# Attention values in two half-width banks, and all key-sample maxima computed in the MLP

## The chip, the cores and the metric

The kernel runs on one core of one Trainium2 chip. The metric is the device time of one execution in microseconds (us). A core has five engines that run side by side, each with its own queue of instructions in order: TensorE (PE in the profile; its weight loads are listed as PEld), VectorE (DVE), ScalarE (ACT), GpSimd (POOL) and SyncE (SP), which here only issues transfers (DMAs). Matmul results land in PSUM, eight banks of 128 partitions by 512 float32 values.

## The reference

`x` has 2048 rows (queries, tokens) of 448 channels. Two branches read it, and a gate per token mixes them.

```python
# A: attention, 16 heads of 28 channels, one shared set of keys and values
q = (x @ wq).reshape(B, S, 16, 28).transpose(0, 2, 1, 3)
k, v = x @ wk, x @ wv
p = softmax(einsum("bhqd,bkd->bhqk", q, k) * 28 ** -0.5)
a = einsum("bhqk,bkd->bhqd", p, v).transpose(0, 2, 1, 3).reshape(B, S, 448) @ wo
# B: shift mixing, then an MLP, each with a residual
h = gelu(layernorm(x) @ w1)               # 448 -> 448, its four quarters shifted by +1 -1 +2 -2 tokens
x1 = x + concat(shifted quarters) @ w2
b = x1 + gelu(layernorm(x1) @ w3) @ w4    # 448 -> 1792 -> 448
g = sigmoid((x * gate_w).sum(-1))
out = g * a + (1 - g) * b
```

## The kernel before

All data are float32. Outside the values and the output projection, a matmul of full precision is made of three faster ones, from a "high" and a "low" part of each operand (names that end in `h` and `l`).

The program runs in three stages, and every engine executes its instructions in the order in which the program text emits them (the schedule is manual; the framework only adds the waits).

**Stage 1** projects queries, keys, values and gate, writes the queries to a DRAM tile `qd`, and computes the shift-mixing half of B.

**Stage 2, the MLP.** Four blocks `b` of 512 tokens; in each, 14 chunks `f` of 128 hidden channels. Chunk `f` runs `w3_part` (11 matmuls of 512 columns, L130 to L134; then two gelus on ScalarE, `gh` L625 and `gf` L626; then `gl = gf - gh` on VectorE, L627) and, from f = 2 on, the four `w4_part` calls of chunk f - 2 (12 matmuls of 448 columns, L635 to L637) into four accumulators. At the end of a block the accumulators are added to `x1` (L693). Between the chunks stand other small jobs: splitting weights, loading keys, layernorm of the next block.

**Stage 3, attention.** Sixteen units `u`: 512 queries by four heads, one head in each quarter of the partitions. A unit has eight steps `v`, each over two tiles `kt` of 128 keys. A step does, in this order on TensorE:
- `scores` of both key tiles: each takes four PSUM banks, one for each head, and fills them in three passes (L800). ScalarE turns each bank into `p = exp(...)` (L810);
- in steps 4 to 7 (`WO_AT`) `wo_job`: the output projection of one quarter of the unit before (L763), added on VectorE (L775);
- `values` of the step before: one bank, 16 passes of 512 columns in four rounds of four (L822), added into `o` by VectorE (L826, L828). Row 0 of each head's result is the sum of its exponentials.

The banks form a ring. `take()` takes the one at the head of the list `banks`, and each is appended at its tail when its reader has been emitted, so an instruction that takes a bank waits for the reader of whoever used it eight takes earlier.

**The shift of the exponentials.** Exponentials are taken of scores minus an estimated maximum. For each unit `max_all` multiplies the queries with 32 sampled keys (`khd`, four matmuls, L203) and reduces on VectorE (L204); `max_end` makes a high and a low part of the negative maxima, transposes them (L227) and writes them with eight small DMAs on SyncE's queue into two spare rows of each head in the query tile `qh` (L231), where the scores' matmul picks them up. The maxima of unit 0 are computed in the MLP (the list `fills`, in the last block), those of unit u + 1 in step 2 of unit u, into a bank of the ring.

**Sums and normalisation.** `sums_begin` reads the sums of a unit in step 0 of the next, `recip` inverts them and spreads them through DRAM with two DMAs, `norm` multiplies `o` by them (L753) ahead of the projection. Queries come from `qd` by `q_load` (L178) and are cast and split by `q_split` (L183, L184).

A tail transposes and normalises the last unit, with a few warm-up matmuls in between. A last, conditional part redoes everything with exact maxima if a sum is out of bounds; it isn't entered here.

Of the kernel before, what the change touches and what calls it, by code (L numbers as in the profile page):

```python
# [9 lines left out]
F32 = mybir.dt.float32  # L10
# [6 lines left out]
P = 128  # L17
# [3 lines left out]
DH = 28  # L21
F = 1792
C = D // 4
NB = S // 512
# [12 lines left out]
def f32(ap):  # L37
    return ap.bitcast(F32)
# [3 lines left out]
def gated_mix_kernel(  # L42
# [44 lines left out]
    def misc_tile(name):  # L87
        return psA.tile([P, 512], F32, tag="misc", bufs=1, name=name)
# [86 lines left out]
    def q_load(u, raw):  # L175
        b, g = divmod(u, NG)
        qr_of[u] = raw
        nc.sync.dma_start(raw, qd[g, :, 512 * b:512 * b + 512])  # L178
# [15 lines left out]
    mx_of = {}  # L194
    mc_of = {}

# [22 lines left out]

    def max_end(u):  # L220
        mr = mx_of.pop(u).rearrange("p j t -> p (j t)")
        mc = late.tile([P, 32], F32R, tag="mc", bufs=1, name=f"mc_{u}")
        nc.vector.tensor_scalar(mc[:, 0:16], mr, -1.0, None, op0=ALU.mult)
        nc.vector.scalar_tensor_tensor(mc[:, 16:32], mr, -1.0, f32(mc)[:, 0:16],
                                       op0=ALU.mult, op1=ALU.subtract)
        mrow = late.tile([P, 32], F32, tag="mrow", bufs=1, name=f"mrow_{u}")
        nc.vector.transpose(mrow, f32(mc))  # L227
        for k in range(2):
            for p in range(4):
                r = 32 * p + 16 * k  # L230
                nc.sync.dma_start(  # L231
                    f32(qh_of[u])[DH + k:P:32, :].rearrange("j (t p q) -> p j t q", p=4, q=32)[p], mrow[r:r + 16, :])

# [368 lines left out]
    with tc.tile_pool(name="s2", bufs=1, reuse_waits="tile") as s2, \  # L602
# [4 lines left out]

        fills = [lambda: max_all(0, misc_tile("m_0")), lambda: max_end(0)]

        def fill():  # L610
            if fills:
                fills.pop(0)()

# [25 lines left out]
        for b in range(NB):  # L639
            acc = [ps2.tile([P, 512], F32, tag="acc", bufs=4, name=f"acc_{b}_{t}") for t in range(4)]  # L640
            gs = {}
            for f in range(NF):
# [28 lines left out]
                if b == 2 and f == 1:  # L671
                    nc.gpsimd.memset(f32(khd), 0.0)
                    for j in range(4):
                        nc.sync.dma_start(f32(khd)[32 * j:32 * j + DH, j, :], f32(kH)[0:DH, 0:MK])
                    q_load(0, s2a.tile([P, 512], F32, tag="xn", bufs=1, name="qr_0"))
                if b == 2 and f == 5:
                    q_split(0, qh0, ql0)
                if f >= 2:
                    for t in range(4):
                        w4_part(f - 2, t, gs[f - 2], acc)  # L680
                        if b > 2 and t % 2 == 0 and f < NF - 1:
                            fill()
            for t in range(4):
# [5 lines left out]
            for t in range(4):  # L689
# [3 lines left out]
                nc.vector.tensor_add(xt, xt, acc[t][:, 0:D])  # L693
        assert not fills
    ctx2.close()


    with tc.tile_pool(name="s3", bufs=1, reuse_waits="tile") as s3, \
# [7 lines left out]
        def take():  # L706
            return banks.pop(0)
# [109 lines left out]
        def values(u, v, add=True):  # L817
            pv = take()
            for kt in (2 * v, 2 * v + 1):
                ps = p_of.pop((u, kt))  # L820
                for j in range(4):
                    nc.tensor.matmul(pv[32 * j:32 * j + 32, :], vext[:, kt, :], ps[j],  # L822
                                     start=(kt % 2 == 0), stop=(kt % 2 == 1), tile_position=(0, 32 * j))
            if v == 0:
                o_of[u] = s3.tile([P, 512], F32, tag="o", bufs=2, name=f"o_{u}")
                nc.vector.tensor_copy(o_of[u], pv)  # L826
            elif add:
                nc.vector.tensor_add(o_of[u], o_of[u], pv)  # L828
            else:
                return pv  # L830
            banks.append(pv)

        READ = (0, 1, 2, 3)
        DRAIN = ()
        WO_AT = (4, 5, 6, 7)
        M_AT = 2

        for k in range(NU * NV):
# [6 lines left out]
            for kt in (2 * v, 2 * v + 1):  # L845
                late_exps(u, kt)
            if v == 2 and sums:
                norms.append(recip(*sums.pop()))
            if v == 3 and norms:
                norm(*norms.pop())  # L850
            if v == M_AT and u + 1 < NU:
                ps = take()
                max_all(u + 1, ps)
                banks.append(ps)
                max_end(u + 1)
            job = None
# [7 lines left out]
            if k:  # L864
                values(*divmod(k - 1, NV))
                if v == 0:
                    sums.append(sums_begin(u - 1, o_of[u - 1]))
        assert not sums and not norms

        u = NU - 1  # L870
        pv = values(u, NV - 1, False)
        o = o_of[u]
        on_of[u] = s3.tile([P, 512], F32, tag="on", bufs=2, name=f"on_{u}")
        toks = [slice(t * P, (t + 1) * P) for t in range(4)]
        tp = [bank(f"ot_{i}").rearrange("p (t n) -> p t n", t=4) for i in range(2)]
        tq = [bank(f"oq_{t}")[:, 0:P] for t in range(4)]
        rr = s3.tile([P, 2, 2, 4], F32, name="rr4")
# [33 lines left out]
        def keep_warm(n):  # L911
            for _ in range(n):
                nc.tensor.matmul(banks[0][:, 0:256], warm[:, 0:P], warm, start=True, stop=True)

        for t in range(4):
            nc.vector.tensor_add(o[:, toks[t]], o[:, toks[t]], pv[:, toks[t]])
        with tc.block():
# [34 lines left out]
        with tc.If(again > 0, label="redo"):  # L952
            for b in range(NB):
                for g in range(NG):
# [3 lines left out]
                    max_full(u, bank)  # L958
                    max_end(u)
                    pv = take()  # L960
# [66 lines left out]
```

## Time and profile before

| | |
|---|---|
| median of 3 runs | 971.56 us (971.14 to 971.71) |
| the profiled execution | 970.74 us, its span 968.9 us |
| TensorE busy | 960.1 us, 99% |
| ScalarE busy | 647.0 us, 67% |
| VectorE busy | 345.7 us, 36% |
| stage 2 starts, stage 3 starts | about 127 us, about 402 us |

The span is the time from the first to the last instruction in the trace. The page's groups give a line, the engine, the operation, the tiles written and read, shapes and count, then busy time and the mean length of one in ns, then the idle time of the engine just ahead of these instructions and what ended it. Rows of the timeline give the start, the length, and in square brackets the idle time before with its releaser; rows of several instructions are merged (xN). A row of the windows view has the stretch, the busy time of PE, PEld, DVE, ACT and POOL with the count of instructions, and then the granted TensorE clock, the share of the DMA engines and GB/s. A row of the waits view has the engine and line that waited, what it waited for, the total in us, how often, and the longest. Matmuls are pipelined, so TensorE shows as busy even where it waits for a bank or an operand: its pace is read from the starts.

### The profile page before, as it was taken

To read this page: it belongs to the slowest core of one execution; us is meant where nothing else is said; L and a number is where in the kernel's file an instruction comes from. 1 tells how busy PE (TensorE), PEld (TensorE's weight loads), DVE (VectorE), ACT (ScalarE), POOL (GpSimd) and SP (SyncE) were. 2 spreads that over 40 slices of the span, in tenths; PEclk is the share of its full clock that TensorE was granted. 3 is DMA by queue.
4 is the path that set the end of the run, shared out by engine and by line. 5 is a ranking of instruction groups with operands and counts; after the bars stand their busy time and mean duration, and the time that the engine had idled before them with its cause. 6 is when DMAs were issued, how large, how long until landed. Compare 5 with 4: busy or idle time off the path is not lost. (4 is left out here: it accounts for less than half of the span.)

```text
span 968.9 us, 19222 instructions
## 1 busy us (share of the span) xinstructions
PE 960.1 (99%) x7571; PEld 589.3 (61%) x7571; DVE 345.7 (36%) x636; ACT 647.0 (67%) x1262; POOL 74.9 (8%) x105
## 2 busy tenths in 40 slices
PE   9999999999999999999999999999999999999996
PEld 7788888888888888644444444444444444444442
DVE  5663354433413421233333333333233332333323
ACT  5532444422222222589999999999999999999993
POOL 2242200221002400200000000000000000000000
PEclk9999999999999999999999999999999999999999
DMA  9703342300300300100000010000010000100001
GB/s 317 263 27 76 103 162 83 89 22 10 93 1 1 82 1 1 60 13 14 14 23 14 24 50 24 14 13 24 24 51 15 14 25 13 53 23 2 13 13 42
DMA packets 38753, 46.22 MB, mean 48 GB/s; under 512 B 8880, under 2 KB 27008, under 8 KB 38656
## 3 DMA queue, kind: packets, MB, share of 16 engines
q1 hardware_dynamic: 35632, 39.45, 13.6%
q10 hardware_dynamic: 3024, 5.47, 1.6%
q8 instruction: 61, 1.00, 0.4%
q14 instruction: 36, 0.29, 0.1%
HBM read 32.85 MB, written 11.67 MB: 46 GB/s over the span
## 5 line engine op out<-in xcount | busy, mean ns | idle before, releaser
L810 ACT ACTIVATE p<-bank 128x512 f32<-128x512 f32 x1024 | 510.9, 653 | 42.7 <-PE bank L800 42.7
L822 PE MATMUL bank<-p,vext 128*32 128x512 f32 x2048 | 245.9, 598 | 0.0
L800 PEld LDWEIGHTS bank<-qh,kH 30*128 30x128 f32 x1024 | 86.2, 182 | 141.8 <-ACT p L810 128.4
L800 PE MATMUL bank<-qh,kH 30*128 30x512 f32 x1024 | 168.4, 465 | 0.1
L625 ACT ACTIVATE gh<-g 128x512 fp32r<-128x512 f32 x55 | 32.8, 597 | 187.6 <-PE g L134 187.6
L800 PE MATMUL bank<-qh,kL 28*128 28x512 f32 x1024 | 137.9, 404 | 0.0
L822 PEld LDWEIGHTS bank<-p,vext 128*32 128x32 f32 x2048 | 59.9, 110 | 127.3 <-issue 101.1
L800 PE MATMUL bank<-ql,kH 28*128 28x512 f32 x1024 | 131.3, 389 | 0.0
L828 DVE TENSOR_TENSOR o<-o,bank 128x512 f32<-128x512 f32 x111 | 76.3, 687 | 123.9 <-PE bank L822 72.9
L627 DVE TENSOR_TENSOR gl<-gf,gh 128x512 fp32r<-128x512 f32 x55 | 38.3, 696 | 168.0 <-ACT gf L626 168.0
L636 PE MATMUL acc<-w4l,gh 128*128 128x448 f32 x220 | 80.4, 366 | 0.0
L635 PE MATMUL acc<-w4h,gh 128*128 128x448 f32 x220 | 80.4, 365 | 0.0
L637 PE MATMUL acc<-w4h,gl 128*128 128x448 f32 x220 | 80.3, 365 | 0.0
L800 PEld LDWEIGHTS bank<-ql,kH 28*128 28x128 f32 x1024 | 73.6, 185 | 9.6
L131 PE MATMUL g<-al,w3h 128*128 128x512 f32 x168 | 65.7, 391 | 0.0
L130 PE MATMUL g<-ah,w3h 128*128 128x512 f32 x168 | 65.6, 390 | 0.0
L132 PE MATMUL g<-ah,w3l 128*128 128x512 f32 x168 | 65.6, 390 | 0.0
L800 PEld LDWEIGHTS bank<-qh,kL 28*128 28x128 f32 x1024 | 62.1, 184 | 0.0
L763 PE MATMUL bank<-wof,on 128*32 128x448 f32 x512 | 61.2, 551 | 0.0
L775 DVE SCALAR_TENSOR_TENSOR ot<-bank,gg,ot 128x448 f32<-128x448 f32 x44 | 30.1, 684 | 85.7 <-PE bank L763 56.9
L635 PEld LDWEIGHTS acc<-w4h,gh 128*128 128x128 f32 x220 | 41.3, 188 | 4.7
L902 POOL TENSOR_TENSOR ot<-y,ot 128x448 f32<-128x448 f32 x1 | 1.2, 1162 | 553.5 <-ACT y L901 553.5
(188 smaller groups left out, 997.1 us busy)
## 6 DMA issues: line engine op xcount, KB each, us to landing
qd<-qf ACTq DMA_DIRECT2D x16, 256.0 KB
qr<-qd SPq DMA_DIRECT2D x16, 256.0 KB
rb<-rd SPq DMA_DIRECT2D x15, 256.0 KB
x<-in_x_dram SPq DMA_DIRECT2D x4, 896.0 KB
xd<-xt SPq DMA_DIRECT2D x16, 224.0 KB
w34raw<-in_w_dram SPq DMA_DIRECT2D x7, 512.0 KB
out_dram<-ot SPq DMA_DIRECT2D x15, 224.0 KB
w34raw<-in_w_dram SPq DMA_DIRECT2D x7, 448.0 KB
```

The costliest lines, as they stand in the source:

```text
L130: nc.tensor.matmul(ps, wh[:, c, :], ah[:, c, :], start=(c == 0), stop=False)
L131: nc.tensor.matmul(ps, wh[:, c, :], al[:, c, :], start=False, stop=False)
L132: nc.tensor.matmul(ps, wl[:, c, :], ah[:, c, :], start=False, stop=False)
L627: nc.vector.tensor_sub(gl, gf, f32(gh))
L635: nc.tensor.matmul(ps, gh[:, tok], w4h[i][:, k, :], start=(f == 0), stop=False)
L636: nc.tensor.matmul(ps, gh[:, tok], w4l[i][:, k, :], start=False, stop=False)
L637: nc.tensor.matmul(ps, gl[:, tok], w4h[i][:, k, :], start=False, stop=(f == stop))
L763: nc.tensor.matmul(ps[32 * j:32 * j + 32, 0:D], on_of[u][:, tok], wof[:, g, :], start=True, stop=True, tile_position=(0, 32 * j))
L800: nc.tensor.matmul(bs[j], w, a, start=(i == 0), stop=(i == 2), tile_position=(32 * j, 0))
L810: nc.scalar.activation(ps[j], bs[j], AF.Exp, scale=SCALE)
L822: nc.tensor.matmul(pv[32 * j:32 * j + 32, :], vext[:, kt, :], ps[j], start=(kt % 2 == 0), stop=(kt % 2 == 1), tile_position=(0, 32 * j))
L828: nc.vector.tensor_add(o_of[u], o_of[u], pv)
```

## The change

Three things change.

1. `values` is done in two halves of 256 queries, each with a PSUM bank of its own, and each half is added into `o` separately. The ring gets one more take per step.
2. All sixteen sets of maxima are computed in the MLP: units 0 to 6 in block 2 at f = 2 to 8, units 7 to 15 in block 3 at f = 0 to 8. For each, the queries are loaded from `qd` (`max_load`) and cast into `qh0` (`max_cast`), behind `w3_part` and ahead of the `w4_part` calls of the chunk; the four matmuls, the reduction and the transpose stand behind these calls. The shift rows are written back into `qd` one chunk later, four DMAs on SyncE's queue and four on ScalarE's, and come with the queries when a unit loads them. Unit 0's own split moves to the end of block 3.
3. `recip` is emitted behind the values of step 1, `norm` behind the values of step 3.

```diff
-    def max_end(u):
+    def max_end(u, again=False):
...
         nc.vector.transpose(mrow, f32(mc))
+        row_of[u] = mrow
+        if again:
+            max_send(u, f32(qh_of[u]), nc.sync)
+
+    def max_send(u, q, other):
+        mrow = row_of.pop(u)
         for k in range(2):
             for p in range(4):
                 r = 32 * p + 16 * k
-                nc.sync.dma_start(
-                    f32(qh_of[u])[DH + k:P:32, :].rearrange("j (t p q) -> p j t q", p=4, q=32)[p], mrow[r:r + 16, :])
+                (other if k else nc.sync).dma_start(
+                    q[DH + k:P:32, :].rearrange("j (t p q) -> p j t q", p=4, q=32)[p], mrow[r:r + 16, :])
...
-        fills = [lambda: max_all(0, misc_tile("m_0")), lambda: max_end(0)]
-
-        def fill():
-            if fills:
-                fills.pop(0)()
+        def max_load(u):
+            if u < NU:
+                q_load(u, s2a.tile([P, 512], F32, tag="xn", bufs=1, name=f"qm_{u}"))
+
+        def max_cast(u):
+            qh_of[u] = qh0
+            nc.vector.tensor_copy(qh0, qr_of.pop(u))
+            max_load(u + 1) if u != 6 else None
...
                         nc.sync.dma_start(f32(khd)[32 * j:32 * j + DH, j, :], f32(kH)[0:DH, 0:MK])
+                    max_load(0)
+                u = f - 2 if b == 2 and 2 <= f <= 8 else f + 7 if b == 3 and f <= 8 else None
+                if b == 2 and f == 12:
+                    max_load(7)
+                if row_of:
+                    w, = row_of
+                    max_send(w, qd[w % NG, :, w // NG * 512:w // NG * 512 + 512], nc.scalar)
+                if u is not None:
+                    max_cast(u)
+                if b == NB - 1 and f == 11:
                     q_load(0, s2a.tile([P, 512], F32, tag="xn", bufs=1, name="qr_0"))
-                if b == 2 and f == 5:
+                if b == NB - 1 and f == 13:
                     q_split(0, qh0, ql0)
                 if f >= 2:
                     for t in range(4):
                         w4_part(f - 2, t, gs[f - 2], acc)
-                        if b > 2 and t % 2 == 0 and f < NF - 1:
-                            fill()
+                if u is not None:
+                    max_all(u, max_tile(f"m_{u}") if u % 2 else misc_tile(f"m_{u}"))
+                    max_end(u)
...
         def values(u, v, add=True):
-            pv = take()
-            for kt in (2 * v, 2 * v + 1):
-                ps = p_of.pop((u, kt))
-                for j in range(4):
-                    nc.tensor.matmul(pv[32 * j:32 * j + 32, :], vext[:, kt, :], ps[j],
-                                     start=(kt % 2 == 0), stop=(kt % 2 == 1), tile_position=(0, 32 * j))
             if v == 0:
                 o_of[u] = s3.tile([P, 512], F32, tag="o", bufs=2, name=f"o_{u}")
-                nc.vector.tensor_copy(o_of[u], pv)
-            elif add:
-                nc.vector.tensor_add(o_of[u], o_of[u], pv)
-            else:
-                return pv
-            banks.append(pv)
+            pvs = []
+            for q in (slice(0, 256), slice(256, 512)):
+                pv = take()
+                for kt in (2 * v, 2 * v + 1):
+                    for j in range(4):
+                        nc.tensor.matmul(pv[32 * j:32 * j + 32, q], vext[:, kt, :], p_of[u, kt][j][:, q],
+                                         start=(kt % 2 == 0), stop=(kt % 2 == 1), tile_position=(0, 32 * j))
+                if v == 0:
+                    nc.vector.tensor_copy(o_of[u][:, q], pv[:, q])
+                elif add:
+                    nc.vector.tensor_add(o_of[u][:, q], o_of[u][:, q], pv[:, q])
+                pvs.append(pv)
+                if add:
+                    banks.append(pv)
+            return pvs
...
-            if v == 2 and sums:
-                norms.append(recip(*sums.pop()))
-            if v == 3 and norms:
-                norm(*norms.pop())
-            if v == M_AT and u + 1 < NU:
-                ps = take()
-                max_all(u + 1, ps)
-                banks.append(ps)
-                max_end(u + 1)
...
             if k:
                 values(*divmod(k - 1, NV))
-                if v == 0:
-                    sums.append(sums_begin(u - 1, o_of[u - 1]))
+            if u and v == 0:
+                sums.append(sums_begin(u - 1, o_of[u - 1]))
+            if u and v == 1:
+                norms.append(recip(*sums.pop()))
+            if u and v == 3:
+                norm(*norms.pop())
```

In the tail the four adds of the last values read the two half banks (`pvs[t // 2]`), and the warm-up matmuls write into a bank of their own.

More of the change, by code (lines that the diff above doesn't have):

```diff
@@ L194, in gated_mix_kernel @@
     mx_of = {}
-    mc_of = {}
+    row_of = {}
     def max_tile(name):
@@ L693, in gated_mix_kernel @@
                 nc.vector.tensor_add(xt, xt, acc[t][:, 0:D])
-        assert not fills
     ctx2.close()
@@ L835, in gated_mix_kernel @@
         WO_AT = (4, 5, 6, 7)
-        M_AT = 2
         for k in range(NU * NV):
@@ L865, in gated_mix_kernel @@
                 values(*divmod(k - 1, NV))
-                if v == 0:
-                    sums.append(sums_begin(u - 1, o_of[u - 1]))
+            if u and v == 0:
[4 more added lines that the diff above has]
+                norm(*norms.pop())
         assert not sums and not norms
         u = NU - 1
-        pv = values(u, NV - 1, False)
+        pvs = values(u, NV - 1, False)
         o = o_of[u]
@@ L875, in gated_mix_kernel @@
         tp = [bank(f"ot_{i}").rearrange("p (t n) -> p t n", t=4) for i in range(2)]
-        tq = [bank(f"oq_{t}")[:, 0:P] for t in range(4)]
+        tq = [bank(f"oq_{t}") for t in range(4)]
+        spare = tq[3]
+        tq = [ps[:, 0:P] for ps in tq]
         rr = s3.tile([P, 2, 2, 4], F32, name="rr4")
@@ L912, in keep_warm @@
             for _ in range(n):
-                nc.tensor.matmul(banks[0][:, 0:256], warm[:, 0:P], warm, start=True, stop=True)
+                nc.tensor.matmul(spare[:, 0:256], warm[:, 0:P], warm, start=True, stop=True)
         for t in range(4):
-            nc.vector.tensor_add(o[:, toks[t]], o[:, toks[t]], pv[:, toks[t]])
+            nc.vector.tensor_add(o[:, toks[t]], o[:, toks[t]], pvs[t // 2][:, toks[t]])
         with tc.block():
@@ L958, in gated_mix_kernel @@
                     max_full(u, bank)
-                    max_end(u)
+                    max_end(u, True)
                     pv = take()
```

## The prediction

> **What bounds the kernel now.** I read the page first (shares by engine, costliest groups), then the order of time in the MLP, then ScalarE's rows in the attention part, then one step of it on all engines.
>
> ```profile
> span 968.9 us, 19222 instructions
> PE 960.1 (99%) x7571; PEld 589.3 (61%) x7571; DVE 345.7 (36%) x636; ACT 647.0 (67%) x1262; POOL 74.9 (8%) x105
> L810 ACT ACTIVATE p<-bank 128x512 f32<-128x512 f32 x1024 | 510.9, 653 | 42.7 <-PE bank L800 42.7
> L822 PE MATMUL bank<-p,vext 128*32 128x512 f32 x2048 | 245.9, 598 | 0.0
> ```
>
> TensorE is busy from end to end, but that means different things. In the MLP its matmuls stand one behind the other with no gap; whatever is put into that stream, or makes it wait, lengthens the run. In the attention part TensorE and ScalarE chase each other: the 1024 exponentials (L810) wait only 42.7 us, always for scores. Its steps are read from where ScalarE starts again:
>
> ```profile
> 885.58 11.92 ACT L810 ACTIVATE p<-bank 128x512 f32<-128x512 f32 x24 [0.43 <-PE bank L800]
> ...
> 906.62 4.03 ACT L810 ACTIVATE p<-bank 128x512 f32<-128x512 f32 x8 [0.70 <-PE bank L800]
> 911.02 4.03 ACT L810 ACTIVATE p<-bank 128x512 f32<-128x512 f32 x8 [0.37 <-PE bank L800]
> 915.46 4.03 ACT L810 ACTIVATE p<-bank 128x512 f32<-128x512 f32 x8 [0.41 <-PE bank L800]
> 919.91 19.87 ACT L810 ACTIVATE p<-bank 128x512 f32<-128x512 f32 x40 [0.42 <-PE bank L800]
> ...
> 949.35 3.04 ACT L810 ACTIVATE p<-bank 128x512 f32<-128x512 f32 x6 [0.42 <-PE bank L800]
> ```
>
> The steps that also project (v 4 to 7) take 4.40 to 4.45 us (906.62, 911.02, 915.46, 919.91) and leave ScalarE idle about 0.4: TensorE binds there. The others are bound by exponentials. One such step on all engines (first scores at 605.29, projection 607.14, values 607.92, the next step's scores 609.75; PEld is the weight load, which TensorE's matmul follows):
>
> ```profile
> 604.79 1.15 ACT L810 ACTIVATE p<-bank 128x512 f32<-128x512 f32 x2
> 605.29 0.19 PEld L800 LDWEIGHTS bank<-qh,kH 30*128 30x128 f32 x4 [0.84 <-ACT p L810]
> 605.50 0.69 DVE L828 TENSOR_TENSOR o<-o,bank 128x512 f32<-128x512 f32 x1 [1.05 <-ACT p L810]
> 606.09 0.66 PE L800 MATMUL bank<-qh,kH 30*128 30x512 f32 x4
> 606.25 0.29 PEld L800 LDWEIGHTS bank<-qh,kL 28*128 28x128 f32 x4
> 607.14 0.16 PEld L763 LDWEIGHTS bank<-wof,on 128*32 128x32 f32 x8 [0.37 <-ACT p L810]
> 607.55 0.13 PEld L822 LDWEIGHTS bank<-p,vext 128*32 128x32 f32 x4 [0.25 <-ACT p L810]
> 607.92 0.13 PEld L822 LDWEIGHTS bank<-p,vext 128*32 128x32 f32 x4 [0.25 <-issue]
> 608.35 0.13 PEld L822 LDWEIGHTS bank<-p,vext 128*32 128x32 f32 x4 [0.30 <-issue]
> 609.75 0.19 PEld L800 LDWEIGHTS bank<-qh,kH 30*128 30x128 f32 x4 [0.84 <-ACT p L810]
> ```
>
> The reader sees two chains that both matter: a bank can be written again only when ScalarE (scores) or VectorE (values) has emptied it, and the next scores stand behind this step's values.
>
> **Part 1, maxima leave the attention part.** The last unit (from 919.91) has no maxima to prepare. It needs 949.35 - 919.91 = 29.44 us to its eighth step; the one before, with maxima, 915.46 - 885.58 = 29.88. So each removal is worth 0.44, and 15 go: **-6.6**. SyncE's eight issues per unit leave too:
>
> ```profile
> 622.04 4.56 SPq L231 DMA_DIRECT2D qh<-mrow  x8
> ```
>
> Nothing waited behind them on that queue that bound, so they add nothing.
>
> **Part 2, maxima enter the MLP.** All 16 now stand there, one per chunk f, at the end of the chunk. The operand is new: the queries are cast into `qh0` on VectorE, and that cast is issued behind `gl` of the same chunk.
>
> ```profile
> 305.26 0.39 PE L130 MATMUL g<-ah,w3h 128*128 128x512 f32 x1
> 309.09 0.69 DVE L627 TENSOR_TENSOR gl<-gf,gh 128x512 fp32r<-128x512 f32 x1 [1.31 <-ACT gf L626]
> 310.20 0.39 PE L130 MATMUL g<-ah,w3h 128*128 128x512 f32 x1
> ...
> 337.12 0.19 PEld L130 LDWEIGHTS g<-ah,w3h 128*128 128x128 f32 x1
> 337.35 0.39 PE L130 MATMUL g<-ah,w3h 128*128 128x512 f32 x1
> 338.67 0.69 DVE L627 TENSOR_TENSOR gl<-gf,gh 128x512 fp32r<-128x512 f32 x1 [3.03 <-ACT gf L626]
> ...
> 339.84 0.39 PE L130 MATMUL g<-ah,w3h 128*128 128x512 f32 x1
> ...
> 342.74 0.61 PEld L203 LDWEIGHTS m<-khd,qh 128*128 128x128 f32 x4
> 343.34 0.42 PE L635 MATMUL acc<-w4h,gh 128*128 128x448 f32 x1
> 345.24 0.40 PE L130 MATMUL g<-ah,w3h 128*128 128x512 f32 x1
> ```
>
> ```profile
> L183 DVE CAST qh<-qr 128x512 fp32r<-128x512 f32 x16 | 6.7, 420 | 5.1 <-DMA qr<-qd 5.1
> ```
>
> An ordinary chunk: 305.26 to 310.20, 4.94. `gl` ends at 309.78, the cast (0.42, with 0.03 between) at 310.23, and TensorE sees it 0.06 later (the add that ends at 606.19 releases a weight load at 606.25): 310.29. The one set of maxima in the MLP now goes from its first weight load to the next matmul in 0.60 (342.74 to 343.34), of which up to 0.20 is the wait behind the matmul before; I take 0.50. So the next chunk starts at 310.79 instead of 310.20: +0.59 (0.49 to 0.69), for 14 chunks, 8.3.
>
> The other two stand in block 3 at f = 0 and 1, where no w4 matmul lies between w3 and the maxima, since these begin at f = 2. There `gl` ends at 339.36, the cast at 339.81, the weight load can go at 339.87, and the next w3 starts at about 340.37 instead of 337.35: +3.02 (2.92 to 3.12) each, 6.0. Unlike before, nothing covers VectorE's chain there: TensorE takes its instructions in order. The set of before goes: 345.24 to 342.74 lies in a chunk that began at 339.84, 0.46 over 4.94. Together **+13.8** (12.2 to 15.4).
>
> What hides the rest: 16 reductions and casts go to VectorE, which idles 1.3 us and more before each `gl`; if that cover went, `gl` would be late next, and it has two chunks. Loads are issued when the cast before is done, so they have nearly a chunk, some 5 us. Between 402.67 and 407.91 one arrived behind the larger `wof`:
>
> ```profile
> 402.67 6.76 SPq L178 DMA_DIRECT2D qr<-qd  x2
> 407.91 0.43 DVE L183 CAST qh<-qr 128x512 fp32r<-128x512 f32 x1 [5.05 <-DMA qr<-qd]
> ```
>
> Alone it is sooner. On SyncE four shift-row writes (4.56/8 = 0.57 each) stand ahead of the next load and end before its cast frees the tile. The four on ScalarE's queue (2.3 us at the same price) fall after the second gelu, where that engine waits 187.6/54 = 3.5 us for the next w3:
>
> ```profile
> ACT gh L625 <- PE g L134: 187.6, 54, 6.7
> ```
>
> The transpose of u waits until the eight writes of u - 1 have landed; next `gl` is more than 1 us later. `q_split(0)` at f = 13 puts 1.1 us on VectorE where it waited 1.23 for the accumulators:
>
> ```profile
> 400.42 2.44 DVE L693 TENSOR_TENSOR x<-x,acc 128x448 f32<-128x448 f32 x4 [1.23 <-PE acc L637]
> ```
>
> **Clock.** Two holes of 2.7 us come into TensorE's stream. How the clock answers to a thin stretch is seen once:
>
> ```profile
> 404.33:407.75 3.42, 3.42 (x22) 1.78 (x23) 0.00 (x0) 3.42 (x8) 2.36 (x2) 1.00 0.83 313
> 407.75:411.16 3.41, 3.41 (x21) 0.60 (x16) 1.12 (x2) 3.33 (x7) 0.00 (x0) 0.50 0.24 54
> ```
>
> In 3.42 us with only 22 matmuls (waiting for exponentials, without a full pause) the clock stayed at 1.00, and the next 3.41 us were granted 0.50. A stretch around one hole would hold even fewer. Such a window costs half of itself, 1.7. I take one: **+1.7** (0 to 3.4). The Trainium skill ("TensorE: Matmul & The Clock Gate", section "What's actually happening") has the half rate after an idle window of about 3.4 us, and its closing table asks for no gaps over about 3; by that, holes of 2.7 cost nothing and the sum is 980.6. The trace halves the clock after a window that was not idle.
>
> **Part 3, values in halves.** Rounds: values run as 4 rounds of 0.43 (607.92, 608.35); now 8 of half length with weights loaded twice as often. A load (0.13) starts with the round and is over long before a half round of 0.215, so it stays hidden. A fixed cost per round is near zero by the 448-column projection round (607.55 to 607.92: 0.37, as its columns to 512), but at most a scores round of 0.23: 0 to 0.10 per step. I take 0.016, nearest the values' own rows; 127 steps: **+2.0** (0 to 12.7).
>
> Banks: what is won is a wait. The fourth bank of the second scores is the one that L828 empties, until 606.19; its load goes at 606.25, some 0.15 behind its fellows (606.09 on). A half-width add would be through earlier: about 0.2 per step once it has passed through three rounds. But the eight banks go round in a ring. A projecting step took 8 + 1 + 1, now 8 + 1 + 2, so the fourth bank of the first scores is no longer that of the sixth exponential of the step before but of the seventh. That one starts at 604.79 and ends (653 ns) at 605.44; its bank is seen at 605.50, 0.21 after 605.29. The fourth chain, begun so late, runs 0.35 and then 0.23 a round and ends within 0.06 of where it ends now; and as TensorE's step shortens, the seventh exponential comes later against it. In the other steps the ring shifts by one as well, but the eighth exponential gates the second scores before and after. I take **0** for the 64 steps (-12.8 to +6.4, from -0.2 to +0.1).
>
> Reciprocals keep their place in VectorE's queue (behind the second step's add); the normalisation goes behind one more add, about 1 us, while the projection that reads it is a step later: 0. **Tail:** four adds (0.88) follow the last values; two may now come earlier, partly beside five warm-up matmuls: **-0.2**.
>
> ```profile
> 954.43 0.72 PE L913 MATMUL bank<-warm 128*128 128x256 bf16 x5
> 954.64 0.88 DVE L916 TENSOR_TENSOR o<-o,bank 128x128 f32<-128x128 f32 x4 [1.05 <-PE bank L822]
> ```
>
> **Sum:** -6.6 + 13.8 + 1.7 + 2.0 + 0 - 0.2 = **+10.7**. The profiled execution took 970.74 (span 968.9 and 1.8 around it), so 981.4; it lies 0.8 under the median of 971.56, and against that it is **982.3**.
>
> **Rivals.** (1) The halved add pays: the ring's new wait doesn't bind, and all 64 projecting steps lose 0.2: -12.8, so 969.5, no slower. For it speaks the 606.25 row; against it the seventh exponential. It decides from 0.14 a step on. (2) Half rounds cost as scores rounds: +10.7 more, 993. Within it, that weight loads are not hidden at all: four more rounds of 0.13 in 127 steps, +66, 1048. The Trainium skill ("TensorE: Matmul & The Clock Gate", section "The mechanism") lets loads overlap running matmuls only in another row group, which would give this; the loads at 607.92 and 608.35 start with the round, so the trace disagrees. (3) The holes don't open, by an earlier cast or later maxima: -5 (two of 2.5), the 14 short waits 1.4 and the clock 1.7 less: 974. (4) The eight small writes land so late that the transpose holds `gl` and the cast: 1 us in 14 chunks, 996.
>
> **Chances.** Forecast 0.65, with its own range of 979 to 987 (clock none or twice, the ends of part 2, 2 more of part 3); (1) 0.12; (2) 0.11, of it 0.02 for exposed loads; (3) 0.07; (4) 0.05. The range of 974 to 992 leaves out most of (1), half of (2) and (4). 0.2% is 1.9 us, about what a measurement of this kernel tells from no change: faster is half of (1), 0.06; same the other half and an edge of (3), 0.07; slower 0.87.
>
> **What would show it.** Right: two gaps of TensorE before the maxima of units 7 and 8 with w3 starts 5.5 apart instead of 2.5; 14 chunks at about 5.5; units of attention shorter by some 0.4; the first scores' fourth load late by 0.2 in projecting steps. Wrong: projecting steps at 4.2, value rounds over 0.22, loads that outlast a chunk.

## Result and profile after

The changed kernel takes 980.98 us (median, 980.45 to 982.22) against 971.35 us (970.56 to 971.71) for the kernel before: ratio 1.0104, 95% interval 1.0088 to 1.0120. The profiled execution took 980.54 us, 9.8 more than that of before. First the lines of its page that answer to those of before (L829 are the exponentials, L844 the values, which now have twice the matmuls of half the width):

```profile
span 978.8 us, 23546 instructions
PE 963.9 (98%) x9619; PEld 660.5 (67%) x9619; DVE 370.4 (38%) x779; ACT 646.7 (66%) x1262; POOL 75.5 (8%) x105
L829 ACT ACTIVATE p<-bank 128x512 f32<-128x512 f32 x1024 | 510.5, 626 | 32.7 <-PE bank L819 32.7
L844 PE MATMUL bank<-p,vext 128*32 128x256 f32 x4096 | 246.3, 381 | 0.0
```

The exponentials wait 10 us less than before (42.7), so the attention part did get shorter; the shares of the engines say nothing of the loss. It shows where one stage is set against the other by the starts of its instructions (first w3 matmul of a block, first exponential of a unit):

| from the two traces, us | before | after | difference |
|---|---|---|---|
| up to the MLP's first w3 matmul | 127.38 | 130.07 | +2.69 |
| MLP, blocks 0 and 1 | 138.29 | 138.29 | 0 |
| block 2 to the first exponential | 137.47 | 154.69 | +17.22 |
| unit 0 | 36.02 | 33.88 | -2.14 |
| units 1 to 14, each | 34.339 | 33.758 | -8.13 in all |
| unit 15 to its eighth step | 29.44 | 29.35 | -0.09 |
| from there to the end | 19.59 | 19.86 | +0.27 |

The first row isn't the change's doing: that code is the same in both, and its length is between 127.4 and 130.3 in the traces below, whatever was changed behind it.

In the MLP, TensorE's rows at the maxima (L203) and at the first w3 matmul behind them: an ordinary chunk with maxima (283.92, then 289.44), and the start of block 3.

```profile
283.92 0.63 PE L203 MATMUL m<-khd,qh 128*128 128x128 f32 x4
284.39 0.45 PE L130 MATMUL g<-ah,w3h 128*128 128x512 f32 x1
...
289.44 0.63 PE L203 MATMUL m<-khd,qh 128*128 128x128 f32 x4
289.91 0.45 PE L130 MATMUL g<-ah,w3h 128*128 128x512 f32 x1
...
346.88 0.63 PE L203 MATMUL m<-khd,qh 128*128 128x128 f32 x4 [2.56 <-DVE qh L620]
347.35 0.61 PE L130 MATMUL g<-ah,w3h 128*128 128x512 f32 x1
...
354.01 0.81 PE L203 MATMUL m<-khd,qh 128*128 128x128 f32 x4 [2.33 <-DVE qh L620]
354.62 0.73 PE L130 MATMUL g<-ah,w3h 128*128 128x512 f32 x1
```

The ordinary chunk takes 289.91 - 284.39 = 5.52, 0.58 more than 4.94. In block 3 TensorE stands still for 2.56 and 2.33 us until VectorE has cast the queries (L620). The same stretch by windows (busy time of PE, PEld, DVE, ACT, POOL with the counts, then clock, DMA share, GB/s):

```profile
344.07:347.48 3.41, 0.85 (x7) 0.63 (x6) 1.25 (x2) 1.08 (x2) 2.39 (x2) 1.00 0.00 0
347.48:350.89 3.41, 3.41 (x10) 2.64 (x10) 1.25 (x4) 0.00 (x0) 0.00 (x0) 0.50 0.29 77
350.89:354.31 3.42, 1.09 (x7) 0.64 (x6) 1.03 (x2) 1.08 (x2) 0.00 (x0) 1.00 0.02 3
354.31:357.72 3.41, 3.41 (x11) 2.73 (x11) 1.25 (x4) 0.00 (x0) 0.00 (x0) 0.50 0.31 78
```

Each window with a hole holds 7 matmuls, and each is followed by one at half the clock, with 10 and 11 matmuls where 3.41 us of the MLP at full clock hold about 16 (281 in the 60 us from 280 on, in the kernel before).

One projecting step of the changed kernel (its projection is L782, its values L844; before's stands in the prediction):

```profile
622.82 1.91 PE L844 MATMUL bank<-p,vext 128*32 128x256 f32 x32
622.82 1.43 PEld L844 LDWEIGHTS bank<-p,vext 128*32 128x32 f32 x28 [0.25 <-issue]
...
624.66 0.41 PEld L819 LDWEIGHTS bank<-qh,kH 30*128 30x128 f32 x4 [0.41 <-ACT p L829]
...
625.00 0.62 PE L819 MATMUL bank<-qh,kL 28*128 28x512 f32 x4
```

The values take 624.66 - 622.82 = 1.84, and before 609.75 - 607.92 = 1.83: eight half rounds cost what four whole ones did. The first scores' four loads now spread over 0.41 instead of 0.19 (the row at 605.29 or 609.75 of before): the fourth comes some 0.2 late.

### The profile page after: what moved, and what is told of

It is laid out like the page before. It is cut to its first block, busy times and chain, and to the rows that moved or that the text cites. A ratio compares the mean times of both kernels' runs of the same rounds, so it can differ in the third digit from the quotient of the medians.

```text
span 978.8 us, 23546 instructions
## 1 busy us (share of the span) xinstructions
PE 963.9 (98%) x9619; PEld 660.5 (67%) x9619; DVE 370.4 (38%) x779; ACT 646.7 (66%) x1262; POOL 75.5 (8%) x105
## 5 line engine op out<-in xcount | busy, mean ns | idle before, releaser
L829 ACT ACTIVATE p<-bank 128x512 f32<-128x512 f32 x1024 | 510.5, 626 | 32.7 <-PE bank L819 32.7
L844 PE MATMUL bank<-p,vext 128*32 128x256 f32 x4096 | 246.3, 381 | 0.0
L844 PEld LDWEIGHTS bank<-p,vext 128*32 128x32 f32 x4096 | 126.4, 110 | 120.2 <-issue 29.3
L819 PE MATMUL bank<-qh,kH 30*128 30x512 f32 x1024 | 187.1, 466 | 0.0
L849 DVE TENSOR_TENSOR o<-o,bank 128x256 f32<-128x256 f32 x222 | 93.5, 421 | 177.5 <-PE bank L844 113.5
L819 PE MATMUL bank<-qh,kL 28*128 28x512 f32 x1024 | 158.4, 407 | 0.0
L819 PE MATMUL bank<-ql,kH 28*128 28x512 f32 x1024 | 147.9, 389 | 0.0
L819 PEld LDWEIGHTS bank<-ql,kH 28*128 28x128 f32 x1024 | 90.2, 185 | 6.9
L819 PEld LDWEIGHTS bank<-qh,kL 28*128 28x128 f32 x1024 | 75.2, 184 | 0.6
L130 PE MATMUL g<-ah,w3h 128*128 128x512 f32 x168 | 67.9, 404 | 0.0
L782 PE MATMUL bank<-wof,on 128*32 128x448 f32 x512 | 61.2, 551 | 0.5
L645 PEld LDWEIGHTS acc<-w4l,gh 128*128 128x128 f32 x220 | 41.3, 188 | 4.2
```

Of the source, the lines that this page charges most:

```text
L130: nc.tensor.matmul(ps, wh[:, c, :], ah[:, c, :], start=(c == 0), stop=False)
L645: nc.tensor.matmul(ps, gh[:, tok], w4l[i][:, k, :], start=False, stop=False)
L782: nc.tensor.matmul(ps[32 * j:32 * j + 32, 0:D], on_of[u][:, tok], wof[:, g, :], start=True, stop=True, tile_position=(0, 32 * j))
L819: nc.tensor.matmul(bs[j], w, a, start=(i == 0), stop=(i == 2), tile_position=(32 * j, 0))
L829: nc.scalar.activation(ps[j], bs[j], AF.Exp, scale=SCALE)
L844: nc.tensor.matmul(pv[32 * j:32 * j + 32, q], vext[:, kt, :], p_of[u, kt][j][:, q], start=(kt % 2 == 0), stop=(kt % 2 == 1), tile_position ...
```

## Experiments

Unit lengths below are means over units 1 to 14 of one profiled execution, or the medians of these units where it says so; they repeat within about 0.02 where nothing was changed, far better than the whole time, because the half-clock windows at the start of the attention part (none, one or two of 3.41 us in the profiles) and the start of the run differ from one profile to the next.

**1. Maxima later in block 3**

```diff
-u = ... f + 7 if b == 3 and f <= 8 else None
+u = ... f + 5 if b == 3 and 2 <= f <= 10 else None
```

> The changed kernel with the maxima of units 7 to 15 at f = 2 to 10 of block 3 instead of f = 0 to 8, so that w4 matmuls stand ahead of every set. Theory (the two holes and their half clock belong to the place f = 0 and 1): the first three chunks of block 3 go from 19.99 back to 10.43 + 0.58 = 11.01, two ordinary chunks get 0.58 each: -7.8, so 973.2 us. Rival 1 (the half clock comes somewhere in block 3 whatever the place, the holes go): -4.4, 976.6. Rival 2 (the excess belongs to units 7 and 8 or to their loads, not to the place): two excesses of 2.6 and 4.2 move to f = 2 and 3, 981.

Measured: 972.93 us (969.47 to 974.49), 1.0013 of before (1.0002 to 1.0024). The first chunks of block 3 are back at 2.53 and 2.49, every chunk with maxima takes 5.46 to 5.54, and block 2 to the first exponential takes 146.23, 8.5 less than in the changed kernel. The theory holds, both rivals fall: nearly the whole loss belonged to two places where TensorE had nothing else to do.

**2. Holes filled with other matmuls**

```diff
+                    if f < 2:
+                        for _ in range(20):
+                            nc.tensor.matmul(ps[:, 0:256], warm[:, 0:P], warm, start=True, stop=True)
                     max_all(u, ps)
```

> The changed kernel with twenty warm-up matmuls (bf16, 256 columns) emitted ahead of the maxima of units 7 and 8, into the PSUM tile that the maxima then overwrite: TensorE is busy in the two holes, which stay as long. Theory (the half clock follows from the holes): the granted clock stays at 1.00 there, two half windows of 1.7 go, 977.6 us, and the first three chunks of block 3 take 16.6 instead of 19.99. Rival 1 (the half clock comes from something else in this stretch, such as the other engines or the DMAs): clock 0.50 as before, 981.0. Rival 2 (the fill itself outlasts the holes): chunks of 5.7 and 7.3 or longer at clock 1.00, 981 or more.

Measured: 976.54 us (975.58 to 977.75). The chunks take 5.71, 5.47 and 5.52, 16.70 together, and the same windows of this run are:

```profile
344.07:347.48 3.41, 3.09 (x26) 2.59 (x24) 1.58 (x3) 1.04 (x2) 2.10 (x2) 1.00 0.00 0
347.48:350.89 3.41, 3.41 (x22) 2.69 (x22) 0.98 (x4) 1.08 (x2) 0.00 (x0) 1.00 0.35 83
350.89:354.31 3.42, 3.38 (x22) 2.74 (x21) 2.07 (x5) 0.00 (x0) 0.00 (x0) 1.00 0.27 74
354.31:357.72 3.41, 3.41 (x18) 2.86 (x18) 1.24 (x3) 1.09 (x2) 0.00 (x0) 1.00 0.04 8
```

The clock stays at 1.00, so the half clock follows from TensorE's standing still. Block 2 to the first exponential takes 151.34, so the clock's part is 154.69 - 151.34 = 3.35 us, and the holes themselves, here filled, are 151.34 - 146.23 (the run before) = 5.11.

**3. The cast ahead of w3**

```diff
+                if u is not None:
+                    max_cast(u)
                 gs[f] = w3_part(b, f)
...
-                if u is not None:
-                    max_cast(u)
```

> The changed kernel with the cast of the queries emitted ahead of w3_part, so that it stands before gl on VectorE. Theory (what makes TensorE wait is the cast that stands behind gl, in all 16 chunks): the two holes and both half-clock windows go (-7.8) and the ordinary chunk falls from 5.52 towards 4.94 + 0.50 = 5.44, fourteen times 0.08 (-1.1): 972.1 us. Rival 1 (the 0.58 of an ordinary chunk is all matmul time, nothing waits there): 973.2. Rival 2 (the maxima wait for something else than gl, the load or khd): 980 to 981.

Measured: 975.50 us (974.16 to 977.55). An ordinary chunk falls to 5.39, below the 5.44 of the theory: a set of maxima costs 0.45 there, so 0.13 of the 0.58 in the changed kernel hang on the later cast. But two other waits took the place of the one removed. At f = 0 and 1 chunks take 3.66 instead of 3.08, because VectorE is still adding the accumulators (L713) and then waits for the load; and in the middle of block 3 chunks take 5.74 to 6.07:

```profile
341.86 0.63 PE L203 MATMUL m<-khd,qh 128*128 128x128 f32 x4 [0.50 <-DVE qh L620]
...
345.52 0.63 PE L203 MATMUL m<-khd,qh 128*128 128x128 f32 x4 [0.46 <-DVE qh L620]
```

```profile
361.38 0.21 DVE L227 STREAM_TRANSPOSE mrow<-mc 128x32 f32<-128x32 f32 x1 [3.30 <-DMA qd<-mrow]
361.51 0.38 DVE L620 CAST qh<-qm 128x512 fp32r<-128x512 f32 x1
...
367.44 0.21 DVE L227 STREAM_TRANSPOSE mrow<-mc 128x32 f32<-128x32 f32 x1 [3.62 <-DMA qd<-mrow]
```

The transpose of one set has to wait until the eight small writes of the set before have left `mrow`, and the next cast stands behind it. That is the prediction's rival 4, which did not bind in the changed kernel and does once the cast is issued earlier. The theory's 972.1 was missed for these two reasons: block 2 to the first exponential takes 148.12, where the theory's sum gives 154.69 - 8.9 = 145.8. The profiled execution (974.30) also has two half-clock windows in unit 0 (36.74 against 33.88); nothing here shows that the edit brought them.

**4. Whole values in the changed kernel, and halves in the kernel before**

```diff
-            for q in (slice(0, 256), slice(256, 512)):
-                pv = take()
+            pv = take()
...
-                        nc.tensor.matmul(pv[32 * j:32 * j + 32, q], vext[:, kt, :], p_of[u, kt][j][:, q],
+                    nc.tensor.matmul(pv[32 * j:32 * j + 32, :], vext[:, kt, :], ps[j],
```

> The changed kernel with whole values (512 columns, one bank, one add, as before), all else as changed: undoes part 3 alone. By the prediction (half rounds cost 0.016 a step, banks nothing, tail -0.2): 981.0 - 2.0 + 0.2 = 979.2 us. By the traces of the two kernels (the unit without maxima in either fell from 29.44 to 29.34, units with maxima by 0.58 where 0.44 was for the maxima, so halves are worth 0.10 to 0.14 a unit, 1.6 to 2.2 in all, and the tail costs 0.4): 982.2 to 982.8. Rival (the halved add pays 0.2 in each projecting step): 993.8.

> The kernel before with the values in halves and nothing else (maxima, reciprocals and normalisation where before has them). The run with whole values in the changed kernel gave units of 33.75 against 33.76 with halves, and a tail 0.25 shorter up to its last adds. Theory from that (round costs, bank gain and ring cost are each near nothing or cancel): units of 34.34 as before, tail +0.25, 971.7 us. The prediction's terms (+2.0 for rounds, 0 for banks, -0.2 tail): 973.3, units of 34.47. Rival (the halved add pays in each projecting step, and only the changed kernel's other parts hid it): 958.7, units of 33.5.

Measured: whole values in the changed kernel 977.79 us (976.30 to 980.11), halves in the kernel before 971.99 us (970.20 to 975.90; 1.0012 of it, 0.9997 to 1.0026). The first number looks as if halves cost 3.2 us. The units don't say so: 33.752 whole and 33.758 halved in the changed kernel; 34.339 whole and 34.353 halved in the kernel before. The four times with whole values fall with the mean granted clock of each execution: 980.11 at 0.991, 978.73 at 0.993, 976.30 and 976.86 at 0.997, while the changed kernel ran at 0.990 to 0.995. So two of them had less half clock than any execution of the changed kernel. A mean of 0.997 over 975 us is 4.9 to 6.8 us at half clock, and the profiles of all these runs spend 2.7 to 4.9 us of that at the very end; that leaves room for one window of 3.41 at most, where the profile of the changed kernel has two at the holes. By this estimate at least one hole went without its half clock there, so the 3.2 us are no price of halves. Halves are worth nothing in the units (+0.2 us over fifteen). The tail is 0.25 longer with them, from the eighth step of the last unit to the start of the last two adds into the output (11.59 against 11.34):

```profile
960.41 4.04 PE L844 MATMUL bank<-p,vext 128*32 128x256 f32 x64
...
964.39 0.72 PE L931 MATMUL bank<-warm 128*128 128x256 bf16 x5
```

The kernel before at the same place:

```profile
950.88 3.62 PE L822 MATMUL bank<-p,vext 128*32 128x512 f32 x32
```

The last two steps' values take 964.39 - 960.41 = 3.98 in halves and 954.43 - 950.88 = 3.55 whole (the warm-up at 954.43 stands in the prediction). A likely reason, not tried by itself: a half runs over both key tiles, so already the first half needs exponentials of the second tile.

The same run also settles what maxima cost in the attention part. Halves in the kernel before and the changed kernel differ there by the maxima and the place of the reciprocals: 34.353 - 33.758 = 0.595 a unit.

**5. The longer ring alone**

```diff
             banks.append(pv)
+            banks.append(take())
```

> The changed kernel with whole values and, in each step, one bank taken and put straight back behind the values, unused: the ring goes round as with halves, but there is no half-width add and no half round. Against the run with whole values (units of 33.75; steps 0 to 3 of 3.84, 4.05, 3.93, 3.94). Theory (the longer ring costs what the earlier half add wins): units longer, by up to 0.2 in each projecting step, 34.0 to 34.5, and 4 to 12 us in all. Prediction (the fourth first-scores bank comes 0.2 late and costs nothing): units of 33.75, no difference. Rival (the pattern of steps 0 to 3 is set by the ring alone): units of 33.76 with steps of 3.93, 3.97, 3.94, 3.96 as in the changed kernel.

Measured: 980.19 us (976.84 to 980.74), units of 33.80 (median of the units; 33.75 with whole values and no extra take), steps 0 to 3 of 3.94, 3.96, 3.95, 3.95 and projecting steps of 4.45 instead of 4.43. So the pattern of steps 0 to 3 is the ring's doing. The ring costs 0.05 a unit, 0.8 us in all, little more than units repeat to; that the earlier half add gives it back (33.76 with both) is the difference of two runs, not shown by itself. The theory's 0.2 in each projecting step isn't there.

The profile of this run also shows that a hole's length alone doesn't set the clock. Its first hole (2.47 us, from 342.13 to 344.60) lies across the border of two windows of 3.41 us (counted back from the half clock that follows), 0.86 in one and 1.62 in the next, and the clock behind both stays at 1.00. Of the second (2.33 us), 2.01 lie in one window, with 1.40 us of matmul time left in it; behind that come two windows at half clock.

**6. Reciprocals and normalisation back**

```diff
+            if v == 2 and sums:
+                norms.append(recip(*sums.pop()))
+            if v == 3 and norms:
+                norm(*norms.pop())
             job = None
```

> The changed kernel with recip back behind the scores of step 2 and norm back behind the scores of step 3, where the kernel before has them; undoes the third part alone. Prediction (the move costs and wins nothing): units of 33.76 and the same time, 980 to 982 us. Rival (the last unit, which has no maxima in either kernel, fell by 0.10 to 0.15 even with whole values, so the move is what wins it): units of 33.87 to 33.91, 1.6 to 2.2 us more.

Measured: 982.30 us (980.81 to 983.29), units of 33.77 (median; 33.76 in the changed kernel). The move is worth nothing here.

**7. Projections spread over all steps**

```diff
-            if v in WO_AT:
-                if u:
-                    job = wo_job(u - 1, WO_AT.index(v))
+            if v < 4:
+                if u > 1:
+                    wo_half(u - 2, v + 4)
...
+            elif u < NU - 1:
+                wo_half(u - 1, v - 4)
```

`wo_half` does 224 of the 448 columns of a projection, with its own bank and its own add; each step has one.

> The kernel before with each unit's four output projections cut into eight halves of 224 columns, one in each step from step 4 of the next unit to step 3 of the one after; maxima and values as before. It tells what bounds the steps: in the changed kernel steps 0 to 3 take 3.95 with TensorE waiting for exponentials (its own work there is 1.80 of scores and 1.84 of values, 3.64) and steps 4 to 7 take 4.42 to 4.69 with ScalarE waiting. Theory (removing work from steps 0 to 3 is worth less than its length because TensorE idles there; work moved into that idle time is cheap): a step costs 3.64 + 0.39 = 4.03 of TensorE everywhere, units of 32.8 to 33.5 instead of 34.34, 13 to 23 us less: 949 to 959 us. Rival 1 (each step is bound by the chain of banks, not by the sum of work): no gain, 969 to 974. Rival 2 (half projections cost as much as whole ones): eight times 0.39 more a unit, 37 to 50 us more.

Measured: 963.25 us (962.04 to 965.47), 0.9908 of before (0.9888 to 0.9927), units of 33.64 (median) instead of 34.34. The theory's direction holds, both rivals fall, but 8 us are won where it gave 13 to 23. Steps take 4.05 to 4.20, the one with maxima 4.78. Units 2, 3 and 4 are longer, their fifth step taking 5.55, 4.51 and 5.14 with the normalisation waiting for its transfer:

```profile
490.87 0.69 DVE L753 TENSOR_TENSOR on<-o,rb 128x512 f32<-128x512 f32 x1 [3.92 <-DMA rb<-rd]
```

**8. Spread projections with the other edits**

The first of these adds the changed kernel's places of recip and norm, and warm-up matmuls in two waits at the start of unit 0; the second is experiment 1 with spread projections and the same warm-up; the third is the second with whole values.

```diff
+            if k == 0:
+                busy(11)
```

> The kernel before with the eight half projections of the run before (963.25 us), and two more edits: recip behind the values of step 1 and norm behind those of step 3 (the places of the changed kernel), and eleven warm-up matmuls each in two waits of TensorE at the start of unit 0. In the run before, the fourth steps of units 2, 3 and 4 took 5.55, 4.51 and 5.14 instead of 4.20, with norm waiting 3.92 for its transfer, and unit 0 had two half-clock windows. Theory (the spread projections need an earlier recip; the half clock at the stage change comes from TensorE's waits): units of 33.6 throughout, no half clock in unit 0 (34 to 35 instead of 37.17): 957 to 960 us. Rival 1 (the move of recip changes nothing, as in the changed kernel; the windows come anyway): 963. Rival 2 (the warm-up matmuls delay the scores that they stand ahead of): unit 0 longer than 37.

> The changed kernel with its maxima at f = 2 to 10 of block 3 (the first run), the eight half projections, and the warm-up matmuls at the start of unit 0. Maxima are in the MLP, values in halves. Theory (a set of maxima costs about the same in both places, 0.58 in a chunk and 0.59 in step 2, and halves cost nothing): as the kernel before with the half projections and early recip, 957 to 961 us, units near 33.0. Rival 1 (with TensorE binding in each step, halves cost their bank: eleven takes in a ring of eight make the scores wait): units of 33.5 or more, 965. Rival 2 (maxima out of step 2 are worth more than 0.6 a unit now that nothing idles there): units under 32.8, 954.

> The run named last (maxima at f = 2 to 10, half projections, warm-up matmuls) with whole values: ten takes a step instead of eleven. Theory (halves are worth nothing in either kernel): within 1 us of it, its tail 0.25 shorter. Rival 1 (the eleventh take binds once each step projects): 3 to 8 us faster. Rival 2 (the half add matters once TensorE binds everywhere): 3 to 6 us slower.

Measured: 960.19 us (959.64 to 960.74), 994.40 us (992.82 to 995.05) and 960.12 us (959.46 to 962.85). The first and the third beat both kernels: 0.9887 (0.9871 to 0.9904) and 0.9896 (0.9879 to 0.9913) of before. With maxima in step 2 units take 33.63, without 33.05 (medians): 0.58, what a chunk of the MLP pays for them. Long fifth steps of units 2 to 4 are gone with the earlier recip. The profiled execution of the first shows no half clock in unit 0; since the changed kernel's shows none there either, without such matmuls, this doesn't prove that they are the reason.

The second is 34 us slower than the third for nothing but halves (units of 35.41 and 33.05, medians). ScalarE's rows show a flat period of 4.43 (708.55, 712.98, 717.41), and the weight loads of the scores show what holds it up:

```profile
708.55 4.03 ACT L852 ACTIVATE p<-bank 128x512 f32<-128x512 f32 x8 [0.40 <-PE bank L838]
712.98 4.03 ACT L852 ACTIVATE p<-bank 128x512 f32<-128x512 f32 x8 [0.40 <-PE bank L838]
717.41 4.03 ACT L852 ACTIVATE p<-bank 128x512 f32<-128x512 f32 x8 [0.40 <-PE bank L838]
```

```profile
711.55 0.28 PEld L838 LDWEIGHTS bank<-qh,kH 30*128 30x128 f32 x3 [0.41 <-ACT p L852]
711.56 1.08 PE L838 MATMUL bank<-qh,kH 30*128 30x512 f32 x4
...
712.14 0.18 PEld L838 LDWEIGHTS bank<-qh,kH 30*128 30x128 f32 x1 [0.31 <-ACT p L852]
712.14 0.29 PEld L838 LDWEIGHTS bank<-qh,kL 28*128 28x128 f32 x4
```

Three heads can load from 711.55 on, the fourth only at 712.14: with eleven takes a step its bank is that of the seventh exponential, which ends at 712.09 in the trace. All later passes stand behind it, and the exponentials wait 0.40 in every step. With ten takes the bank is that of the sixth, the four heads load together, and the same steps take 4.08 to 4.18:

```profile
700.90 0.25 PEld L838 LDWEIGHTS bank<-qh,kH 30*128 30x128 f32 x4 [0.84 <-ACT p L852]
```

**9. Both halves in one bank**

```diff
+            pv = take()
             for q in (slice(0, 256), slice(256, 512)):
-                pv = take()
```

> The run with half projections in every step and values in halves (994.4 us, units of 35.41, steps of 4.43), with both halves of the values in one bank: half rounds and half adds stay, the eleventh take goes. Theory (the longer ring alone binds there: the fourth bank of the first scores is that of the seventh exponential): units of 33.0 as with whole values, 960.3 us with the tail's 0.25. Rival 1 (half rounds cost once TensorE binds): units over 34, 975 or more. Rival 2 (the earlier, shorter half add wins without the ring's price: the step with TensorE waiting 0.20 for the bank falls towards 4.03): units of 32.3 to 32.8, 950 to 957 us.

Measured: 1053.29 us (1053.13 to 1054.25), units of 38.97 (median). It tells nothing of the ring, since another wait took over:

```profile
740.96 0.42 DVE L872 TENSOR_TENSOR o<-o,bank 128x256 f32<-128x256 f32 x1 [0.51 <-PE bank L867]
741.43 0.59 PEld L867 LDWEIGHTS bank<-p,vext 128*32 128x32 f32 x16 [1.08 <-DVE o L872]
741.44 1.07 PE L867 MATMUL bank<-p,vext 128*32 128x256 f32 x16 [0.60 <-DVE o L872]
```

The second half's matmuls wait in every step until VectorE has read the first half out of the same bank. The Trainium skill ("PSUM — Partial Sum Buffer", section "PSUM bank collisions raise a hardware error") has it that a bank must be guarded as a whole, not by address, within 32 partitions; the trace shows such a guard, one of the waits that the framework adds, and its price, 0.60 of TensorE a step. Under this guard halves need banks of their own, and that is what lengthens the ring. That the ring and not the half add makes the 4.43 therefore rests on the row at 712.14, not on this run; the longer ring alone wasn't tried with half projections.

## Why the prediction was right, and where not

982.3 was forecast and 980.98 measured. By terms, against its sum of +10.7:

- **Maxima leave: -6.6 forecast, -8.9 measured** (0.595 in fifteen units). The step that was mis-sized is the 0.44, taken from 29.88 against 29.44. The last unit of before was no good sample of a unit without maxima: the same unit takes 29.28 in the changed kernel with whole values, where no unit prepares maxima. In the kernel before its first four steps take 4.04, 3.84, 4.04 and 3.92 instead of 3.84, 4.04, 3.93 and 3.96, and the next three are 0.09 longer together; why is open. Compared in whole units the removal is worth 0.59.
- **Maxima enter: +13.8 forecast, +13.9 measured** with the clock held up (151.34 - 137.47). An ordinary chunk is 0.58 longer (0.59 forecast); the two holes were 2.56 and 2.33 long where 2.7 was forecast, and cost 5.1.
- **Clock: +1.7 forecast, +3.35 measured**, two windows, the upper end. By the Trainium skill's rule ("TensorE: Matmul & The Clock Gate", section "What's actually happening") holes of 2.7 would have cost nothing; the trace disagrees, since 2.56 and 2.33 us each halved the clock of the window behind. That the rule's 980.6 lies next to the measured time is chance, as the next lines show. The two windows are those of the profiled execution; a hole that falls across two windows can go without (experiments 4 and 5).
- **Half rounds: +2.0 forecast, +0.2 measured** (units with halves against whole ones, so together with the banks), at the lower bound. Rival 2 falls with it.
- **Banks: 0 forecast, 0 measured**, and by what the traces show for the reason given: the fourth load of the first scores is 0.2 late as forecast, and a longer ring alone costs 0.8 us. What a half add would win without the longer ring no run shows. Rival 1 falls. The condition named there ("as TensorE's step shortens, the seventh exponential comes later against it") became, by the row at 712.14, a cost of 34 us in the run with shorter projecting steps.
- **Reciprocals and normalisation: 0 forecast, 0 measured.** In these runs the earlier place mattered only where projections were spread (experiments 7 and 8).
- **Tail: -0.2 forecast, +0.25 measured.** What was left out is that the last values can get longer when cut into halves (3.98 against 3.55).

The measured terms make -8.9 + 13.9 + 3.35 + 0.2 + 0.25 = +8.8. The profiled executions differ by 9.8: the changed one also started the MLP 2.7 later, and it lacked the half-clock window at the start of unit 0 that the profile of before has (about -1.6). Neither belongs to the change: the profiles have none to two windows there in kernels of either kind. So errors of size (2.3 too little won, 1.8 too much for rounds, against 1.7 too little lost to the clock and 0.45 at the tail) cancelled within 2 us. The mechanisms were right, in the MLP above all; that the sum came so close is partly luck.

One reading of the prediction is wrong without a term hanging on it: 4.40 to 4.45 are steps 5 to 7. Step 4, the first that projects, takes 4.8 in the kernel before (901.81 to 906.62) and 4.69 in the changed one.

Rival 3, that the holes don't open, was priced at 974; made to happen, it gives 972.9.

## What to carry to other kernels

Work moved into a stage whose bounding engine is busy throughout costs its full length and what it waits for (0.45 and 0.13 here), so the move pays only if it cost more where it stood (0.59, so it won nothing); the place in the instruction order decides the rest, and a set of matmuls that waits for a chain on another engine belongs behind other matmuls. Where steps alternate between two bounding engines, spreading the same work evenly (projections in every step) won 8 us, and 11 with the earlier reciprocal and the warm-up matmuls; moving the maxima out won nothing. Count the takes of a ring of buffers before adding one: which reader the next writer waits for shifts with it, and the eleventh take went with a cost of 0.8 us in one schedule and, by the row that waits, of 34 us in another.

## What was not expected of the hardware

Holes of 2.56 and 2.33 us were enough to halve TensorE's clock for the following 3.41 us, and twenty small matmuls in each prevented it. Each of these holes lay within one window; a hole of 2.47 us that lay across two, 0.86 and 1.62, cost no clock. With whole values, whose holes are about as long (2.37 and 2.33), two of four executions had a mean clock of 0.997, too high for half clock at both holes, and the others 0.991 and 0.993. So what half-clock windows fall on differs between executions of one program. Comparing the lengths of units within the traces resolved 0.02 us where medians were uncertain by 2 to 3.
